# FFN chunks of 502 and 500 columns over the batch border, with attention's result in one DRAM array

## Chip, cores and metric

The kernel runs on one core of a Trainium2 chip. The metric is the device time of one execution in microseconds. A run of the kernel before is the median of three executions; one further execution was profiled.

## What is computed

```python
# u, v: 2 x 3008 x 256; z: 2 x 3008 x 64
scores = (1.0 / S) * np.matmul(z, z.transpose(0, 2, 1))
attn = np.maximum(scores, 0.0) ** 2
x = (u * np.matmul(attn, v)).reshape(B * S, D)      # 6016 x 256
h = np.maximum(x @ moe_w_in, 0.0)                   # 256 -> 2048
x = h * h @ moe_w_out                               # 2048 -> 256
h = x @ moe2_w_in
y = (h - np.tanh(h)) @ moe2_w_out
```

All arrays are float32 in the reference, and the weights arrive as float64. The kernel holds tokens along the free dimension (it reads `u` transposed and writes `y` transposed).

## The kernel before

Every product is computed as three products of a high and a low part: an operand is rounded to the matrix format (`h`), the rest is subtracted (`l`), and TensorE adds high x high, low x high and high x low in PSUM. So each product of a 128-row weight block with a chunk of tokens is three matmuls, each with its own weight load of 128 columns.

**Chunks.** `qch` cuts the 3008 tokens of a batch into five chunks of 512 columns and one of 448. `chunks` lists them for both batches, `NCH` = 12 in all; chunks 5 and 11 (counted from 0) have 448 columns. In the kernel before this list serves attention and the FFNs alike.

**Attention.** For each chunk, 12 steps `("att", c, x)` compute scores, ReLU, square and the product with `v`. `take` adds the result up into an SBUF tile, and `keep` (L482) stores it to a DRAM scratch tile `xd[c]`. For chunk 0 (`EARLY` = 1) `gate` multiplies by `u` before the store; for the others the product with `u` is made after the load, in `split_x`.

**FFNs.** Each FFN has 16 steps per chunk, one for each 128 columns of its hidden dimension: `("m1", c, k)` and `("m2", c, k)`. A step has a front and a back. `front` (L493) is six matmuls (three products over two halves of the 256 features) into a PSUM tile `s`. Between them ScalarE and VectorE compute the nonlinear function and split its result: for m1 `bend` (L519), `power` (L522), `high` (L565 on ScalarE or L567 on VectorE) and `rest` (L570); for m2 `shape` (L528), `bend` (L519), `shape2` (L531), `differ` (L536), `mask` (L547 on VectorE), `times` (L555), `pick` (L558), `high` and `rest`. `back` (L572) is six matmuls of the result into two PSUM tiles `o` that collect all 16 steps. With 12 chunks, 32 steps and 12 matmuls each there are 4608 matmuls in the FFNs.

After its 16 steps an m1 chunk is split into the operand of m2 by `between`, and an m2 chunk is copied out by `out` and stored by `send`. The very last half chunk is copied and stored in two pieces by `send_last` (L630 to L633), one on ScalarE's DMA queue.

**Order.** m1 runs 41 steps ahead of m2 at first (`lead`); later the lead shrinks to 21, and after the last m1 step the last 21 m2 steps stand alone. In these `mask` runs on ScalarE (`alone`, L543). On TensorE the order is written out: the fronts run `LOOK` = 3 steps ahead of the backs, and `FAR` = 4 after the last m1 step. For the other engines and for the SP queue a planner fixes the order while the program is built: each piece of work is a `Job` with a due time, a cost, what it must follow and the buffers it takes, and `drive` always takes the next by these. The due times come from `plan`, which adds up TensorE's times. The order is therefore static, and it depends on the costs that the planner is given. In the kernel before the line that gives the FFN's six matmuls their time is

```python
t += 0.68 * size(i) if kind == "s" else 1.36 if size(i) == 1 else 1.22
```

**Loads for the FFNs.** `load_x` (L262) reads a chunk back from `xd` into a tile of the pool `xp` (two buffers, shared with the output tile `y`); `load_u` (L300) brings its `u`. Their due times lie 16 us before the chunk's first front (`need - 16.0`), and the load may not be issued before that chunk's `keep`.

Of the kernel before, what the change touches and what calls it, by code (L numbers as in the profile page):

```python
# [9 lines left out]
F32 = mybir.dt.float32  # L10
# [7 lines left out]
P = 128  # L18
NMAX = 512
# [12 lines left out]
EARLY = 1  # L32
# [10 lines left out]
def kernel(  # L43
# [22 lines left out]
    B, DQK, S = zT.shape  # L66
    D = v.shape[2]
    DFF = w1_in.shape[1]
    KD = D // P
# [7 lines left out]
    NC = len(qch)  # L77
    chunks = [(b, q, n) for b in range(B) for q, n in qch]
    NCH = len(chunks)
    NV = KB // 2  # L80

    wp = ctx.enter_context(tc.tile_pool(name="wp", bufs=NW))
# [8 lines left out]
    dp = ctx.enter_context(tc.tile_pool(name="dp", bufs=1, space=bass.MemoryType.DRAM))  # L91
# [5 lines left out]
    V, A, T, SP = nc.vector, nc.scalar, nc.tensor, nc.sync  # L97
# [20 lines left out]
    steps = [("att", c, x) for c in range(NCH) for x in range(NV)]  # L118
# [16 lines left out]
    xt = {}  # L135
# [2 lines left out]
    nc.gpsimd.memset(ebias, -float(896 << 23))  # L138
    lbias = cp.tile([P, 1], F32, name="lbias")
    nc.gpsimd.memset(lbias, (TC * math.tanh(TB * TH)) ** 2)  # L140
    xd = dp.tile([NCH, P, KD, NMAX], F32, name="xd")
    wd = dp.tile([KEEP0 + KEEP1, P, 2, 512], F32, name="wd")
    ad = {
        (b, t, k): dp.tile([4, P, 4, P], F32, name="ad")
# [115 lines left out]
        return xs[m, c]  # L260

    def load_x(c):  # L262
        n = chunks[c][2]
        x = xp.tile([P, KD, NMAX], F32, tag="x", name="xr")
        SP.dma_start(out=x[:, :, :n], in_=xd[c, :, :, :n])
        return x

    def split_x(c, x, u):
        n = chunks[c][2]
        if c >= EARLY:  # L270
            yield "V", lambda: V.tensor_mul(x[:, :, :n], x[:, :, :n], u[:, :, :n])
        xh, xl = new_xs(0, c)
        yield "A", lambda: A.activation(xh[:, :, :n], x[:, :, :n], AF.Copy)
        for k in range(KD):
            yield "V", lambda k=k: V.tensor_sub(xl[:, k, :n], x[:, k, :n], xh[:, k, :n])


    order = [(m, f) for m in range(2) for f in range(NF)]
    keeps = {STAY + k: k for k in range(KEEP0 + KEEP1)}
    split = STAY + KEEP0 + KEEP1  # L280
# [16 lines left out]
        k = p % 2 * 2 + g  # L297
        return z[:, k * P : (k + 1) * P]

    def load_u(c, u):  # L300

        b, q, n = chunks[c]
        t0 = b * S + q
        SP.dma_start(
            out=u[:, :, :n],
            in_=uT[:, t0 : t0 + n].rearrange("(k p) t -> p k t", p=P),
        )
# [173 lines left out]

    def keep(c):  # L482

        n = chunks[c][2]
        x = xt.pop(c) if c < EARLY else sums[c]
        SP.dma_start(out=xd[c, :, :, :n], in_=x[:, :, :n])

    def ask_u(c):

        xt[c] = xp.tile([P, KD, NMAX], F32, tag="x", name="x")  # L490
        load_u(c, xt[c])

    def front(i):  # L493
        kind, c, k = steps[i]
        n = chunks[c][2]
        if not single:
            s_pool.close()
            single["s"] = ctx.enter_context(
                tc.tile_pool(name="pf", bufs=4, space=bass.MemoryType.PSUM)
            )  # L500
        s = got[i] = single["s"].tile([P, NMAX], F32, tag="s", name="s")
        m = 0 if kind == "m1" else 1
        w = wt["w", m, k]
        xh, xl = xs[m, c]
        seq = [(hl, mv, kd) for hl, mv in ((0, xh), (1, xh), (0, xl)) for kd in range(KD)]
        for j, (hl, mv, kd) in enumerate(seq):
            T.matmul(  # L507
                s[:, :n],
                lhsT=w[:, hl, kd * P : (kd + 1) * P],
                rhs=mv[:, kd, :n],  # L510
                start=j == 0,
                stop=j == len(seq) - 1,
            )

    def bend(i, func):

        n = chunks[steps[i][1]][2]
        a = sq[i] = ap_.tile([P, NMAX], F32, tag="a", name="a")[:, :n]
        A.activation(a, got[i][:, :n], func)  # L519

# [2 lines left out]

    def shape(i):

        n = chunks[steps[i][1]][2]
        f = gs[i] = fs[i] = tp.tile([P, NMAX], F32, tag="t", name="f")[:, :n]
        A.activation(f, got[i][:, :n], AF.Tanh, scale=TB)  # L528

# [2 lines left out]

    def differ(i):

        n = chunks[steps[i][1]][2]
        V.tensor_sub(sq[i], got[i][:, :n], sq[i])  # L536

    def mask(i, alone):

        n = chunks[steps[i][1]][2]  # L540
        if alone:
            small = zp.tile([P, 2, KD, NMAX], F32, tag="z", name="least")[:, 0, 0, :n]
            A.activation(small, fs[i], AF.Relu, scale=-1.0, bias=lbias)  # L543
            least[i] = small.bitcast(U32)
        else:
            small = least[i] = mp.tile([P, NMAX], U8, tag="small", name="small")[:, :n]
            V.tensor_scalar(small, fs[i], limit, None, op0=ALU.is_lt)  # L547

    def times(i, alone):

        n = chunks[steps[i][1]][2]
        f = fs[i]
        if alone:
            gs[i] = tp.tile([P, NMAX], F32, tag="t", name="g")[:, :n]
        V.tensor_mul(gs[i], got[i][:, :n], f)  # L555
# [3 lines left out]

    def high(i, e, pool):  # L560

        n = chunks[steps[i][1]][2]
        pair[i] = pool.tile([P, 2, NMAX], F32R, tag="h" if pool is hp else "w", name="h")[:, :, :n]
        if e == "A":
            A.activation(pair[i][:, 0], sq[i], AF.Copy)  # L565
        else:
            V.tensor_copy(pair[i][:, 0], sq[i])  # L567
# [3 lines left out]

    def back(i):  # L572
        kind, c, k = steps[i]
        n = chunks[c][2]
        if k == 0:
            acc[kind, c] = [po.tile([P, NMAX], F32, tag="o", name="o") for _ in range(KD)]
        o = acc[kind, c]
        w = wt["w", 0 if kind == "m1" else 1, k]
        h, l = pair[i][:, 0], pair[i][:, 1]
        seq = [(t, d) for t in ((0, h), (1, h), (0, l)) for d in range(KD)]  # L580
        if k in (0, NF - 1):
            seq.sort(key=lambda x: x[1])
        for j, ((side, mv), d) in enumerate(seq):
            T.matmul(  # L584
                o[d][:, :n],
                lhsT=w[:, side, (KD + d) * P : (KD + d + 1) * P],
                rhs=mv,
                start=k == 0 and j % 3 == 0,
                stop=k == NF - 1 and j % 3 == 2,
            )  # L590

    def between(c, d, e):

        n = chunks[c][2]
        if d == 0 and e == "A":
            new_xs(1, c)
        xh, xl = xs[1, c]
        o = acc["m1", c][d][:, :n]
        if e == "A":
            A.activation(xh[:, d, :n], o, AF.Copy)  # L600
        else:
            V.tensor_sub(xl[:, d, :n], o, xh[:, d, :n])

    def out(c, d, e):

        n = chunks[c][2]
        if d == 0:
            xt["y", c] = xp.tile([P, KD, NMAX], F32, tag="x", name="y")
        y, o = xt["y", c][:, d, :n], acc["m2", c][d][:, :n]
        if e == "A":  # L610
            A.activation(y, o, AF.Copy)
        else:
            V.tensor_copy(y, o)

    def send(c):

        b, q, n = chunks[c]
        t0 = b * S + q
        SP.dma_start(
            out=yT[:, t0 : t0 + n].rearrange("(k p) t -> p k t", p=P),  # L620
            in_=xt["y", c][:, :, :n],
        )

    def send_last():

        c = NCH - 1
        b, q, n = chunks[c]
        t0 = b * S + q
        y, o = xt["y", c], acc["m2", c]
        SP.dma_start(out=yT[:P, t0 : t0 + n], in_=y[:, 0, :n])  # L630
        for way, cols in ((A, slice(0, n // 2)), (SP, slice(n // 2, n))):
            V.tensor_copy(y[:, 1, cols], o[1][:, cols])  # L632
            way.dma_start(out=yT[P:, t0 : t0 + n][:, cols], in_=y[:, 1, cols])  # L633
# [136 lines left out]
    def span(kind, i):  # L770
# [2 lines left out]
            return whole  # L773
        return whole * (share if kind == "o" else 1 - share)

    def plan(first_steps):

        order_p, ahead = [], 2
# [18 lines left out]
                ahead += 1  # L797
            order_p.append(("b", n))
        when, t = {}, 0.0
        size = lambda i: chunks[steps[i][1]][2] / NMAX  # L800
        for kind, i in order_p:
            when[kind, i] = t
            if kind[0] == "o":
                t += size(i) * span(kind, i)
            else:
                t += 0.68 * size(i) if kind == "s" else 1.36 if size(i) == 1 else 1.22
        vjob, zjob, blocks = {}, {}, {}
        zhold = {(b, t): hold("z") for b in range(B) for t in range(0, NC, 2)}
        vhold = {(b, j): hold("w") for b in range(B) for j in range(NV)}
# [31 lines left out]
        for b in range(B):  # L841
            base = b * NC * NV
            for j in range(NV):
# [7 lines left out]
                if b == 0 and j in v_loaded:  # L851
                    raw[0] = v_loaded[j]
                    room[pool].pop(0)
                    after = [(asked[0], 3.0 + 0.5 * j)]
                else:
# [4 lines left out]
                    after = [(load, 0.0)]  # L860
# [84 lines left out]
        for c in range(NCH):  # L945
# [8 lines left out]
            def ask2(e, pools, c=c, u=u):  # L954
                pool = homes[pools[0]]
                u[0] = pool.tile([P, KD, NMAX], F32, tag=pools[0], name="u")
                load_u(c, u[0])
            after = [(asks, 0.0), (("keep", c), 0.0)]
            after = [(Job(ask, need - 16.0, after, ["x"], [xs_], S=2.6), 0.0)]
            X = [("A", 1.06), ("V", 0.69), ("V", 0.69)]  # L960
            give = [(2, xs_)]
# [23 lines left out]
    def forward(kind, c, k, when, size, wjob, whold, xjob, xhold):  # L985
# [2 lines left out]
        m, f = int(kind == "m2"), size(i)  # L988
        alone = i > at["m1", NCH - 1, NF - 1]
        need = when["b", i]  # L990
        part = 1.36 if f == 1 else 1.22
        s_, a, t_, small, hs = hold("f"), hold("a"), hold("t"), hold("z" if alone else "small"), hold(None)
        after = [(wjob[m, k], 0.0), *xjob[m, c]]
        if i == at["m1", 0, 0]:
# [62 lines left out]
        y = hold("x")  # L1057
# [208 lines left out]
```

## Time and profile before

| | us |
|---|---|
| median of three executions | 1474.54 |
| lowest and highest of the three | 1474.37 and 1474.82 |
| the profiled execution, whole | 1474.81 |
| its span, first to last instruction | 1473.0 |

The profiled execution is thus 0.27 us above the median, and 1.81 us of it lie outside the span. The span has attention in its first part and the FFNs from about 442 us on. TensorE's row in the profile counts overlapping matmuls as one busy time and models their ends, so its work is read here from start times: the distance from one matmul's start to the next one's.

### The profile page before, as it was taken

The numbers are of one execution on the slowest core, as the hardware profiler recorded it, in microseconds if no ns is written. First come the engines' busy times: TensorE is split into PE (matmuls) and PEld (weight loads), VectorE is DVE, ScalarE is ACT, GpSimd is POOL, SyncE is SP. The second block draws the span as 40 slices with busy tenths as digits, with TensorE's granted clock in tenths as the row PEclk, the third lists the DMA queues.
The fourth block names the chain that finished last, engine by engine and source line by source line (L and its number), as shares of the span: only waits on it lengthen the run. The fifth ranks groups of instructions, "written<-read, shape, count | busy, mean of one in ns | idle before, by whom it ended". The sixth has DMA issues, their size and how long they took to land.

```text
span 1473.0 us, 21953 instructions
## 1 busy us (share of the span) xinstructions
PE 1467.4 (100%) x8512; PEld 1232.4 (84%) x8512; DVE 1230.8 (84%) x1837; ACT 1078.8 (73%) x1712; POOL 0.3 (0%) x6
## 2 busy tenths in 40 slices
PE   9999999999999999999999999999999999999999
PEld 7888888888898888888888888888888888888888
DVE  7888999788986888877888888887888878888888
ACT  8987659987648987666667667677766766666688
POOL 0000000000000000000000000000000000000000
PEclk9999999999999999999999999999999999999999
DMA  8756548765663330010100100010101010000000
GB/s 247 254 191 221 208 154 259 268 219 211 216 243 103 111 95 35 1 40 1 44 1 0 44 1 15 1 44 1 41 1 43 1 40 1 15 1 1 15 1 28
DMA packets 71784, 125.67 MB, mean 85 GB/s; under 512 B 4736, under 2 KB 52224, under 8 KB 67840
## 3 DMA queue, kind: packets, MB, share of 16 engines
q1 hardware_dynamic: 71376, 123.90, 24.8%
q8 instruction: 66, 1.08, 0.3%
q10 hardware_dynamic: 304, 0.38, 0.1%
q14 instruction: 38, 0.31, 0.1%
HBM read 75.24 MB, written 49.02 MB: 84 GB/s over the span
## 4 chain that ended last, share of the span: by engine, by line
PE 99%; DMA 1%; SPq 0%; DVE 0%; issue 0%; DVEq 0%
PE o L584 35%; PE s L507 35%; PE o L458 25%; PE s L421 4%; DMA vraw<-in_v_dram 0%; DMA zraw<-in_z_dram 0%; SPq L180 0%; SPq L160 0%; DVE l L363 0%; DVE vw L173 0%; DVE y L632 0%; DVEq L1262 0%
## 5 line engine op out<-in xcount | busy, mean ns | idle before, releaser
L584 PE MATMUL o<-h,ww 128*128 128x512 f32 (+1 forms) x2304 | 575.6, 385 | 0.0
L507 PE MATMUL s<-xs,ww 128*128 128x512 f32 (+1 forms) x2304 | 575.2, 385 | 0.0
L584 PEld LDWEIGHTS o<-h,ww 128*128 128x128 f32 x2304 | 432.3, 188 | 81.4 <-DVE h L570 0.3
L507 PEld LDWEIGHTS s<-xs,ww 128*128 128x128 f32 x2304 | 432.4, 188 | 81.3 <-issue 0.3
L458 PE MATMUL o<-h,vw 64*128 64x512 f32 (+1 forms) x2256 | 341.4, 382 | 0.2 <-ACT vw L172 0.2
L519 ACT ACTIVATE a<-s 128x512 f32<-128x512 f32 (+1 forms) x384 | 225.1, 586 | 153.4 <-PE s L507 152.1
L570 DVE TENSOR_TENSOR h<-a,h 128x512 fp32r<-128x512 f32 (+1 forms) x384 | 249.4, 677 | 28.3 <-ACT h L565 24.6
L458 PEld LDWEIGHTS o<-h,vw 64*128 64x128 f32 x2256 | 211.4, 184 | 40.5 <-ACT vw L172 0.7
L536 DVE TENSOR_TENSOR a<-s,a 128x512 f32<-128x512 f32 (+1 forms) x192 | 130.3, 679 | 109.4 <-ACT a L519 109.0
L458 PE MATMUL o<-l,vw 64*128 64x512 f32 (+1 forms) x1128 | 215.5, 383 | 0.4 <-DVE l L363 0.4
L528 ACT ACTIVATE f<-s 128x512 f32<-128x512 f32 (+1 forms) x192 | 112.9, 588 | 106.6 <-PE s L507 105.5
L565 ACT ACTIVATE h<-a 128x512 fp32r<-128x512 f32 (+1 forms) x230 | 142.0, 619 | 22.0 <-PE o L584 10.7
L558 DVE COPY_PREDICATED a<-small,f 128x512 f32<-128x512 uint8 (+1 forms) x171 | 126.8, 742 | 5.2
L458 PEld LDWEIGHTS o<-l,vw 64*128 64x128 f32 x1128 | 105.4, 184 | 21.8 <-DVE l L363 1.7
L522 ACT ACTIVATE a<-a 128x512 f32<-128x512 f32 (+1 forms) x192 | 119.5, 622 | 5.3
L329 DVE STREAM_TRANSPOSE at<-m 128x1024 f32<-128x1024 f32 x60 | 121.4, 2023 | 0.0
L555 DVE TENSOR_TENSOR f<-s,f 128x512 f32<-128x512 f32 (+1 forms) x171 | 117.0, 684 | 5.1
L531 ACT ACTIVATE f<-f 128x512 f32<-128x512 f32 (+1 forms) x192 | 120.1, 626 | 0.0
L363 DVE TENSOR_TENSOR l<-a,h 128x1024 fp32r<-128x1024 f32 (+1 forms) x83 | 100.5, 1214 | 20.7 <-ACT h L354 20.3
L354 ACT ACTIVATE h<-at 128x1024 fp32r<-128x1024 f32 (+1 forms) x60 | 61.4, 1023 | 47.7 <-PE o L458 42.2
L385 ACT ACTIVATE a<-a 128x1024 f32<-128x1024 f32 (+1 forms) x83 | 87.3, 1053 | 1.3
L374 ACT ACTIVATE a<-s 128x1024 f32<-128x1024 f32 x79 | 80.0, 1014 | 6.7 <-PE s L421 6.3
(56 smaller groups left out, 801.7 us busy)
## 6 DMA issues: line engine op xcount, KB each, us to landing
ad<-a SPq DMA_DIRECT2D x60, 512.0 KB, 3.9
m<-ad SPq DMA_DIRECT2D x30, 1024.0 KB, 6.7
wraw<-in_moe_w_in_dram SPq DMA_DIRECT2D x32, 256.0 KB, 3.9
wraw<-in_moe_w_out_dram SPq DMA_DIRECT2D x32, 256.0 KB, 4.1
vraw<-in_v_dram SPq DMA_DIRECT2D x22, 256.0 KB, 5.0
wd<-wk SPq DMA_DIRECT2D x10, 512.0 KB, 3.8
ww<-wd SPq DMA_DIRECT2D x10, 512.0 KB, 9.2
xr<-xd SPq DMA_DIRECT2D x10, 512.0 KB, 4.7
```

The source lines that it names most:

```text
L329: V.transpose(a.rearrange("p g (k j m) -> p m k g j", k=4, m=4), m.rearrange("p (m k) (t g i) -> t p m k g i", m=4, t=2, g=2)[p % 2],)
L458: T.matmul(o[r * KD + d][:, :n], lhsT=w[halves[r], hl, g * D + d * P : g * D + (d + 1) * P], rhs=mv[halves[r], g, :n], start=x == 0 and (r ...
L507: T.matmul(s[:, :n], lhsT=w[:, hl, kd * P : (kd + 1) * P], rhs=mv[:, kd, :n], start=j == 0, stop=j == len(seq) - 1,)
L519: A.activation(a, got[i][:, :n], func)
L522: A.activation(sq[i], sq[i], AF.Square)
L531: A.activation(fs[i], fs[i], AF.Square, scale=TC)
L536: V.tensor_sub(sq[i], got[i][:, :n], sq[i])
L555: V.tensor_mul(gs[i], got[i][:, :n], f)
L558: V.copy_predicated(sq[i], least[i], gs[i])
L565: A.activation(pair[i][:, 0], sq[i], AF.Copy)
L570: V.tensor_sub(pair[i][:, 1], sq[i], pair[i][:, 0])
L584: T.matmul(o[d][:, :n], lhsT=w[:, side, (KD + d) * P : (KD + d + 1) * P], rhs=mv, start=k == 0 and j % 3 == 0, stop=k == NF - 1 and j % 3 ...
```

## The change

The FFNs get a chunking of their own. `groups` cuts the 6016 tokens of both batches together into twelve chunks: eight of 502 columns and four of 500. The sixth group (tokens 2510 to 3011) lies over the batch border at 3008. Attention keeps its chunks of 512 and 448.

The scratch `xd` becomes one array over all tokens. `keep` writes an attention chunk into its columns, `load_x` reads a group's columns; a group's load now follows the `keep` of every attention chunk that it touches. Since chunk 0 is already multiplied by `u` and covers 512 tokens, group 1 leaves out its first 10 columns in that product. The planner's time for six FFN matmuls becomes a formula of the width.

```diff
+    assert B * S % 2 == 0
+    even = [2 * (B * S // 2 // NCH + (c < B * S // 2 % NCH)) for c in range(NCH)]
+    groups = [(sum(even[:c]), n) for c, n in enumerate(even)]
+
+    def width(kind, c):
+        return chunks[c][2] if kind == "att" else groups[c][1]
...
-    xd = dp.tile([NCH, P, KD, NMAX], F32, name="xd")
+    xd = dp.tile([P, KD, B * S], F32, name="xd")
...
     def load_x(c):
-        n = chunks[c][2]
+        t0, n = groups[c]
         x = xp.tile([P, KD, NMAX], F32, tag="x", name="xr")
-        SP.dma_start(out=x[:, :, :n], in_=xd[c, :, :, :n])
+        SP.dma_start(out=x[:, :, :n], in_=xd[:, :, t0 : t0 + n])
...
         if c >= EARLY:
-            yield "V", lambda: V.tensor_mul(x[:, :, :n], x[:, :, :n], u[:, :, :n])
+            y = slice(max(done_u - t0, 0), n)
+            yield "V", lambda: V.tensor_mul(x[:, :, y], x[:, :, y], u[:, :, y])
...
     def keep(c):
-        n = chunks[c][2]
+        b, q, n = chunks[c]
+        t0 = b * S + q
         x = xt.pop(c) if c < EARLY else sums[c]
-        SP.dma_start(out=xd[c, :, :, :n], in_=x[:, :, :n])
+        SP.dma_start(out=xd[:, :, t0 : t0 + n], in_=x[:, :, :n])
...
     def front(i):
         kind, c, k = steps[i]
-        n = chunks[c][2]
+        n = groups[c][1]
...
+    def ffn(f):
+        return 0.08 + 1.28 * f
...
-        size = lambda i: chunks[steps[i][1]][2] / NMAX
+        size = lambda i: width(*steps[i][:2]) / NMAX
...
-                t += 0.68 * size(i) if kind == "s" else 1.36 if size(i) == 1 else 1.22
+                t += 0.68 * size(i) if kind == "s" else ffn(size(i))
...
-                load_u(c, u[0])
-            after = [(asks, 0.0), (("keep", c), 0.0)]
+                load_u(*groups[c], u[0])
+            t0, n = groups[c]
+            after = [(asks, 0.0)]
+            for k, (b, q, m) in enumerate(chunks):
+                if t0 < b * S + q + m and b * S + q < t0 + n:
+                    after.append((("keep", k), 0.0))
...
-        part = 1.36 if f == 1 else 1.22
+        part = ffn(f)
```

The other functions of the FFNs (`bend` to `rest`, `back`, `between`, `out`, `send`, `send_last`) take their width, and the last two their tokens, from `groups` in the same way.

## Rows read from the trace of the kernel before

**Rows 1.** The page's busy times by engine, and the granted clock by slice.

```profile
PE 1467.4 (100%) x8512; PEld 1232.4 (84%) x8512; DVE 1230.8 (84%) x1837; ACT 1078.8 (73%) x1712; POOL 0.3 (0%) x6
...
PEclk9999999999999999999999999999999999999999
```

**Rows 2.** The page's chain that ended last, by engine.

```profile
PE 99%; DMA 1%; SPq 0%; DVE 0%; issue 0%; DVEq 0%
```

**Rows 3.** Instructions of lines 507 and 584: count, durations (ns), first and last start (us).

```profile
L507 PE MATMUL s<-xs,ww x2304: 362/389/506, 442.0 to 1462.9; 128*128 128x512 f32 x157, 128*128 128x448 f32 x35
...
L584 PE MATMUL o<-h,ww x2304: 362/389/468, 447.6 to 1469.2; 128*128 128x512 f32 x157, 128*128 128x448 f32 x35
```

**Rows 4.** TensorE's timeline where all FFN chunks have 512 columns: start, length, six matmuls each.

```profile
599.94 1.52 PE L584 MATMUL o<-h,ww 128*128 128x512 f32 x6
...
610.82 1.52 PE L584 MATMUL o<-h,ww 128*128 128x512 f32 x6
```

**Rows 5.** The same timeline in the last chunk, 448 columns alone.

```profile
1436.35 1.38 PE L584 MATMUL o<-h,ww 128*128 128x448 f32 x6
...
1461.89 1.38 PE L507 MATMUL s<-xs,ww 128*128 128x448 f32 x6
```

**Rows 6.** Weight loads of line 507 over the span: busy time, mean ns, idle before.

```profile
L507 PEld LDWEIGHTS s<-xs,ww 128*128 128x128 f32 x2304 | 432.4, 188 | 81.3 <-issue 0.3
```

**Rows 7.** TensorE's timeline where chunks of 448 and 512 columns alternate.

```profile
765.86 1.52 PE L584 MATMUL o<-h,ww 128*128 128x512 f32 x6
767.22 1.38 PE L507 MATMUL s<-xs,ww 128*128 128x448 f32 x6
768.43 1.54 PE L584 MATMUL o<-h,ww 128*128 128x512 f32 x6
769.82 1.52 PE L507 MATMUL s<-xs,ww 128*128 128x512 f32 x6
```

**Rows 8.** Timeline at the FFNs' start, all engines.

```profile
442.04 5.75 PE L507 MATMUL s<-xs,ww 128*128 128x512 f32 x24
...
447.62 1.52 PE L584 MATMUL o<-h,ww 128*128 128x512 f32 x6
```

**Rows 9.** Busy us of PE, PEld, DVE, ACT, POOL by stretch, then clock, DMA, GB/s.

```profile
560.00:760.00 200.00, 200.00 (x884) 165.58 (x884) 161.54 (x270) 135.84 (x236) 0.00 (x0) 1.00 0.05 18
...
1422.00:1462.00 40.00, 40.00 (x194) 36.17 (x194) 39.62 (x74) 39.38 (x81) 0.00 (x0) 1.00 0.04 14
```

**Rows 10.** Groups of two operations over 1422 to 1462 us, by form.

```profile
L558 DVE COPY_PREDICATED a<-least,g 128x448 f32<-128x448 uint32 x14 | 9.6, 682 | 0.0
L543 ACT ACTIVATE least<-f,lbias 128x448 f32<-128x448 f32 x14 | 9.5, 677 | 0.3
...
L558 DVE COPY_PREDICATED a<-least,g 128x512 f32<-128x512 uint32 x3 | 2.3, 761 | 0.0
L543 ACT ACTIVATE least<-f,lbias 128x512 f32<-128x512 f32 x3 | 2.2, 729 | 0.0
```

**Rows 11.** Timeline of the last 6 us; in brackets the idle time before and its releaser.

```profile
1467.69 1.53 PEld L584 LDWEIGHTS o<-h,ww 128*128 128x128 f32 x8 [0.34 <-DVE h L570]
...
1469.63 0.69 DVE L632 COPY y<-o 128x224 f32<-128x224 f32 x2 [1.17 <-PE o L584]
1470.06 0.35 ACTq L633 DMA_DIRECT2D out_dram<-y  x1
1470.35 0.34 SPq L633 DMA_DIRECT2D out_dram<-y  x1
```

**Rows 12.** The stores of line 486: count, issue durations (ns), first and last start (us).

```profile
L486 SPq DMA_DIRECT2D xd<-e x11: 319/320/596, 89.9 to 443.4; - x11
```

**Rows 13.** DMA issues by form: count, KB each, median us to landing.

```profile
xr<-xd SPq DMA_DIRECT2D x10, 512.0 KB, 4.7
out_dram<-y SPq DMA_DIRECT2D x10, 512.0 KB, 3.1
...
out_dram<-y SPq DMA_DIRECT2D x1, 112.0 KB, 1.9
```

More of the change, by code (lines that the diff above doesn't have):

```diff
@@ L275, in split_x @@
             yield "V", lambda k=k: V.tensor_sub(xl[:, k, :n], x[:, k, :n], xh[:, k, :n])
+    done_u = sum(n for _, _, n in chunks[:EARLY])
     order = [(m, f) for m in range(2) for f in range(NF)]
@@ L298, in keys, with load_u @@
         return z[:, k * P : (k + 1) * P]
-    def load_u(c, u):
-        b, q, n = chunks[c]
-        t0 = b * S + q
+    def load_u(t0, n, u):
         SP.dma_start(
@@ L482, in keep @@
     def keep(c):
-        n = chunks[c][2]
+        b, q, n = chunks[c]
+        t0 = b * S + q
         x = xt.pop(c) if c < EARLY else sums[c]
-        SP.dma_start(out=xd[c, :, :, :n], in_=x[:, :, :n])
+        SP.dma_start(out=xd[:, :, t0 : t0 + n], in_=x[:, :, :n])
     def ask_u(c):
         xt[c] = xp.tile([P, KD, NMAX], F32, tag="x", name="x")
-        load_u(c, xt[c])
+        b, q, n = chunks[c]
+        load_u(b * S + q, n, xt[c])
     def front(i):
         kind, c, k = steps[i]
-        n = chunks[c][2]
+        n = groups[c][1]
         if not single:
@@ L515, in bend @@
     def bend(i, func):
-        n = chunks[steps[i][1]][2]
+        n = width(*steps[i][:2])
         a = sq[i] = ap_.tile([P, NMAX], F32, tag="a", name="a")[:, :n]
@@ L524, in shape @@
     def shape(i):
-        n = chunks[steps[i][1]][2]
+        n = width(*steps[i][:2])
         f = gs[i] = fs[i] = tp.tile([P, NMAX], F32, tag="t", name="f")[:, :n]
@@ L533, in differ @@
     def differ(i):
-        n = chunks[steps[i][1]][2]
+        n = width(*steps[i][:2])
         V.tensor_sub(sq[i], got[i][:, :n], sq[i])
     def mask(i, alone):
-        n = chunks[steps[i][1]][2]
+        n = width(*steps[i][:2])
         if alone:
@@ L549, in times @@
     def times(i, alone):
-        n = chunks[steps[i][1]][2]
+        n = width(*steps[i][:2])
         f = fs[i]
@@ L560, in high @@
     def high(i, e, pool):
-        n = chunks[steps[i][1]][2]
+        n = width(*steps[i][:2])
         pair[i] = pool.tile([P, 2, NMAX], F32R, tag="h" if pool is hp else "w", name="h")[:, :, :n]
@@ L573, in back @@
         kind, c, k = steps[i]
-        n = chunks[c][2]
+        n = groups[c][1]
         if k == 0:
@@ L592, in between @@
     def between(c, d, e):
-        n = chunks[c][2]
+        n = groups[c][1]
         if d == 0 and e == "A":
@@ L604, in out @@
     def out(c, d, e):
-        n = chunks[c][2]
+        n = groups[c][1]
         if d == 0:
@@ L615, in send @@
     def send(c):
-        b, q, n = chunks[c]
-        t0 = b * S + q
+        t0, n = groups[c]
         SP.dma_start(
@@ L626, in send_last @@
         c = NCH - 1
-        b, q, n = chunks[c]
-        t0 = b * S + q
+        t0, n = groups[c]
         y, o = xt["y", c], acc["m2", c]
@@ L956, in ask2 @@
                 u[0] = pool.tile([P, KD, NMAX], F32, tag=pools[0], name="u")
-                load_u(c, u[0])
-            after = [(asks, 0.0), (("keep", c), 0.0)]
+                load_u(*groups[c], u[0])
+            t0, n = groups[c]
+            after = [(asks, 0.0)]
+            for k, (b, q, m) in enumerate(chunks):
+                if t0 < b * S + q + m and b * S + q < t0 + n:
+                    after.append((("keep", k), 0.0))
             after = [(Job(ask, need - 16.0, after, ["x"], [xs_], S=2.6), 0.0)]
```

## The prediction

> **What bounds the kernel now.** I read the page first. TensorE is busy for practically the whole span, at full granted clock in every slice; VectorE and ScalarE are not [rows 1]. The chain of waits says the same from the other end: 99% of it is TensorE [rows 2]. So the time is the sum of the matmuls' own times plus the few places where TensorE waits, and the change can gain only by making matmuls cheaper or removing such places. It concerns the FFNs' 4608 matmuls alone.
>
> The lengths in TensorE's rows are modelled, so I read distances between starts. The FFNs' first matmul starts at 442.0 and the last at 1469.2 [rows 3]; with 0.2 for the last one itself the FFNs hold TensorE for 1027.4 us. To see what that is made of I asked for TensorE's timeline in three kinds of stretch.
>
> Where all chunks have 512 columns, eight groups of six matmuls lie between the first row and the last: (610.82 - 599.94) / 48 = 226.67 ns each [rows 4]. At the granted clock of 1.00, the 2.4 GHz level [rows 9], 512 columns are 213.33 ns, so 13.33 ns per matmul are not columns.
>
> In the last chunk, with 448 columns alone, 21 groups lie between the rows: (1461.89 - 1436.35) / 126 = 202.70 ns [rows 5]. The same composition would give 448 / 2.4 + 13.33 = 200.00. What is longer there is the weight load. It lasts 188 ns whatever the chunk [rows 6], and 188 + 14.7 = 202.7: under a matmul of 448 columns it no longer fits. Under one of 512 it has 226.67 - 188 = 38.7 ns to spare.
>
> Where the two widths alternate, a chunk of 448 also taxes its neighbour. A group of six 512s that follows one of 448 takes 769.82 - 768.43 = 1.39 us, while the group before the 448s took 767.22 - 765.86 = 1.36 [rows 7].
>
> **The change part by part.** *Twelve even chunks instead of ten wide and two narrow.* The number of matmuls stays 4608 and the columns stay 384 x 6016. If a matmul costs columns / 2.4 + 13.33 ns, the FFNs cost 384 x 6016 / 2.4 = 962.56 us, plus 4608 x 13.33 = 61.44, together 1024.0, however the tokens are cut. The kernel before is 3.4 above this line. Of that, 768 matmuls of 448 columns make 768 x 2.70 = 2.07. The start makes 0.14: the first 24 matmuls take 447.62 - 442.04 = 5.58 instead of 5.44 [rows 8]. The end makes about 0.3, where the weight loads wait for VectorE's `h` [rows 11]. The rest, 0.9, I put down to the neighbours of [rows 7].
>
> At 500 and 502 columns the line gives 221.67 and 222.50 ns. The weight load then has 33.7 ns to spare, near the 38.7 at which no excess shows, and far from the 448s. So the 2.07 and the 0.9 go. The start and the end stay. New sum: 1024.0 + 0.14 + 0.34 = 1024.5, a gain of 2.9.
>
> The width itself does not occur in the trace, so I bound it from the two that do. If nothing of a matmul were fixed, its price would be 226.67 / 512 per column. At the mean width of 501.33 that is 221.94 ns, and 1022.7 us in all: 1.3 less than the line. If the price lay on the straight line between the two measured widths it would be 202.70 + 53.33 x 23.97 / 64 = 222.67, and 1026.1 in all: 2.1 more. I take the line of fixed part and clock between them, since the 448s are explained by the weight load and so say little about the slope.
>
> *The end of the kernel.* The last chunk grows from 448 to 500 columns. After the last matmul stand two copies of half a chunk and their stores [rows 11]. The copies take 0.69 for 224 columns each; 250 columns make it 0.69 x 250 / 224 = 0.77, so +0.08. The last store moves 125 KB instead of 112. It lands in 1.9 us [rows 13], so between nothing and 0.2 more. I take 0.02, because an output of 512 KB lands in 3.1. Together +0.1.
>
> *VectorE and ScalarE.* While m1 and m2 steps alternate they have room: 162 and 136 of 200 us [rows 9], and 502 columns are less work than 512. In the last 21 m2 steps, which stand alone, they have none: 39.6 and 39.4 of 40 [rows 9]. There, from 448 to 500 columns `pick` grows by 52 x (761 - 682) / 64 = 64 ns or 9%, and `mask` by 42 ns or 6% [rows 10]. TensorE's matmul grows from 202.70 to 221.67, by 9%. So the engines keep pace as they do now, and I cost this at nothing. The cover is TensorE's own lead of four fronts. Were it used up, what comes late is the next `back`, and the price is the second rival.
>
> *Moved loads and stores.* No DMA is added. `keep` writes rows of 2 KB into the array instead of 4 KB. The last one is issued at 443.4 [rows 12] and, by the store of equal size, lands some 3 us later [rows 13]. Only the last two groups need it. The first group needs chunk 0's `keep` alone, as before, and the sixth those of three chunks that were stored hundreds of us earlier. Were a group's load to wait for a store that it does not need, SP's queue behind it, with the weights' loads, would stand for those 3 us. Loads are due 16 us ahead and land in 4.7 [rows 13], so that hides it. Without that cover it would cost 3 us once.
>
> A rule that speaks against the change concerns these rows. Off a 512-column grid, a group's rows start at multiples of 2008 bytes. The Trainium skill, "DMA: Bandwidth & Descriptors", section "How a descriptor splits into AXI transactions", says that a piece which does not start on a 256-byte boundary also fetches the bytes before it. Estimated from that page, the last rows' 1000 bytes cost 33 beats, where the 896 bytes of before cost 28. No row here shows an unaligned piece of this kind. By the page the last store's data would take up to 18% longer, which stays inside the 0.2 allowed for it, and the loads keep their cover.
>
> *Sum.* -2.9 + 0.1 = -2.8 us. The profiled execution took 1474.81 us with a span of 1473.0, and this makes it 1472.0 with a span of 1470.2. That execution is 0.27 above the median, so the forecast for the median is 1474.54 - 2.8 = **1471.7 us**. That is 0.19% less. About 0.2% (2.95 us) is what a measurement of this kernel can tell from no change, so the forecast lies just inside that limit.
>
> **Rivals.**
>
> *The array works in steps of columns.* Both measured widths are multiples of 64, so the trace can't exclude that 502 and 500 columns are charged as the next multiple of something. With a step of 16 or more both cost what 512 does: 4608 x 226.67 = 1044.5, which is 20.5 above the line and gives 1492.2, slower by 1.2%. From a step of 16 on this decides the sign; with a step of 8 (504 columns for both, 223.33 ns) it is 1029.1, so 5.1 more and 1476.8; with 4, 1474.3. Nothing in the rows speaks for it. Against it speaks only that 512 columns need no more than their clocks plus a small remainder. The Trainium skill, "TensorE: Matmul & The Clock Gate", section "Wait — 56ns, not 53.3ns?", gives a matmul's distance as columns over the clock plus 2.5 ns, without steps. The trace differs in the constant (13.3), and no run here shows a width off the grid.
>
> *The last steps, or a new static order, stall TensorE.* The planner gets new costs and so may set another order. Both helpers are full in the last 52 us, and the kernel before already ends with 0.34 us of waiting for `h` [rows 9, 11]. If each of the 21 steps came late by a tenth of its 2.66 us, that is 5.6 us and 1477.3; half of that gives 1474.5. Against it: 162 of 200 before that stretch, and equal growth in it.
>
> *The narrow chunks were not the cause.* If price per column between 448 and 512 is a straight line, the 2.07 us stay and only the neighbours' tax goes: 1471.7 + 2.1 = 1473.8, no change to be told. The weight load's 188 ns speak against it.
>
> **How the numbers follow.** The forecast's own case, a smooth price per column and no new stall, gets 0.78; within it the time lies from 1470.4 to 1472.7. Its fixed part decides whether it passes the 0.2% limit, at 1471.6: I give 0.43 to faster and 0.35 to same. A column step of 16 or more gets 0.05 (slower), of 4 or 8 together 0.05 (same). The stalls get 0.08, of which 0.06 same and 0.02 slower. The straight line gets 0.04 (same). Together: faster 0.43, same 0.50, slower 0.07. The range must leave out no more than 0.2. I take 1470.2 to 1474.3; this holds the forecast's case, the straight line, a step of 4 and the small stalls.
>
> **What would show it.** Right: starts of matmuls 221.7 and 222.5 ns apart through all of the FFNs, no group of 1.39 us, first to last start near 1023.9 + 0.4, and attention's part as before, its last matmul near 442. Wrong: 226.7 or 223.3 ns per matmul; weight loads or matmuls waiting for `h` in the last 50 us for more than 0.5 us; TensorE waiting for an `xs` of a new group; or a last store that lands later than 2.1 us.

## The result, and the profile after

The changed kernel takes 1483.23 us (median of six, 1482.62 to 1483.81), the kernel before in the same runs 1474.68. The ratio is 1.0059, with a 95% interval of 1.0048 to 1.0070: slower by 8.6 us, where 2.8 less was forecast and the range ended at 1474.3. Three executions in the experiments below ran at a granted clock of 0.62 to 0.85, among them the profiled ones of `e3_array_only` and `e7_narrow_last`; the ratios leave them out, and no row of their traces is used.

The page of the changed kernel, busy times and chain, says what it said before [rows 1, 2]: TensorE is the bound.

```profile
PE 1474.8 (100%) x8512; PEld 1232.5 (83%) x8512; DVE 1237.9 (84%) x1851; ACT 1072.1 (72%) x1698; POOL 0.3 (0%) x6
...
PE 98%; DMA 1%; DVE 0%; SPq 0%; issue 0%; ACT 0%; DVEq 0%
```

The FFNs' matmuls (now lines 516 and 593), with first and last start:

```profile
L516 PE MATMUL s<-xs,ww x2304: 382/385/502, 441.4 to 1469.6; 128*128 128x502 f32 x125, 128*128 128x500 f32 x67
...
L593 PE MATMUL o<-h,ww x2304: 382/388/498, 446.9 to 1477.1; 128*128 128x502 f32 x125, 128*128 128x500 f32 x67
```

From first to last start the FFNs take 1035.7 us, against 1027.2 before [rows 3]. They begin 0.6 earlier, and after the last start stand 4.2 us instead of 3.8. 8.5 - 0.6 + 0.4 = 8.3 is the difference of the two spans (1481.3 and 1473.0). The 0.6 is no work of the change: in the whole kernels below, which all keep attention as it is, this start lies anywhere from 441.1 to 442.2. So the loss is in the FFNs, and TensorE's timeline shows it in stretches without any waiting. Groups of six matmuls, first with 502 columns throughout, then where 502 and 500 alternate, then with 500:

```profile
599.68 1.50 PE L593 MATMUL o<-h,ww 128*128 128x502 f32 x6
...
610.40 1.50 PE L593 MATMUL o<-h,ww 128*128 128x502 f32 x6
...
1147.74 1.50 PE L593 MATMUL o<-h,ww 128*128 128x502 f32 x6
1149.09 1.51 PE L516 MATMUL s<-xs,ww 128*128 128x500 f32 x6
1150.44 1.56 PE L593 MATMUL o<-h,ww 128*128 128x502 f32 x6
1151.83 1.56 PE L516 MATMUL s<-xs,ww 128*128 128x502 f32 x6
1153.23 1.51 PE L593 MATMUL o<-h,ww 128*128 128x500 f32 x6
...
1299.86 1.52 PE L593 MATMUL o<-h,ww 128*128 128x500 f32 x6
...
1310.74 1.52 PE L593 MATMUL o<-h,ww 128*128 128x500 f32 x6
```

(610.40 - 599.68) / 48 = 223.33 ns for 502 columns, and (1310.74 - 1299.86) / 48 = 226.67 ns for 500. The narrower matmul is the dearer one and costs exactly what 512 columns did [rows 4]. Where the two alternate, most groups take 1.34 to 1.36 us. But behind a single group of 500 columns, as the one at 1149.09, the next groups of 502 take 1.39 and 1.40 us, the latter 1.40 / 6 = 233 ns per matmul. That happens behind nine of the ten such single groups, to 19 groups of 502, and costs 1.1 us in all.

The end, in the same order as [rows 11]:

```profile
1474.01 3.02 PEld L593 LDWEIGHTS o<-h,ww 128*128 128x128 f32 x14 [0.78 <-DVE h L579]
1474.01 3.45 PE L593 MATMUL o<-h,ww 128*128 128x500 f32 x14 [0.36 <-DVE h L579]
...
1477.49 0.74 DVE L639 COPY y<-o 128x250 f32<-128x250 f32 x2 [1.45 <-PE o L593]
1477.94 0.35 ACTq L640 DMA_DIRECT2D out_dram<-y  x1
1478.27 0.34 SPq L640 DMA_DIRECT2D out_dram<-y  x1
```

The weight loads wait 0.78 us for `h` (0.34 before). The copies take 0.74 (0.69). By the DMA issues the last store lands after 2.2 us instead of 1.9, and the loads of `x` after 5.0 instead of 4.7 [rows 13]:

```profile
xr<-xd SPq DMA_DIRECT2D x8, 502.0 KB, 5.0
...
out_dram<-y SPq DMA_DIRECT2D x1, 125.0 KB, 2.2
```

### The profile page after: what moved, and what is told of

Its sections match the earlier page's. It is cut to its first block, busy times and chain, and to the rows that moved or that the text cites. A ratio compares the mean times of both kernels' runs of the same rounds, so it can differ in the third digit from the quotient of the medians.

```text
span 1481.3 us, 21975 instructions
## 1 busy us (share of the span) xinstructions
PE 1474.8 (100%) x8512; PEld 1232.5 (83%) x8512; DVE 1237.9 (84%) x1851; ACT 1072.1 (72%) x1698; POOL 0.3 (0%) x6
## 4 chain that ended last, share of the span: by engine, by line
PE 98%; DMA 1%; DVE 0%; SPq 0%; issue 0%; ACT 0%; DVEq 0%
PE s L516 35%; PE o L593 35%; PE o L465 25%; PE s L428 4%; DMA vraw<-in_v_dram 0%; DMA zraw<-in_z_dram 0%; SPq L187 0%; DVE vw L180 0%; DVE l L370 0%; DVE z L204 0%; SPq L167 0%; DVE a L567 0%; DVE h L579 0%; ACT f L537 0%; DVE g L564 0%
## 5 line engine op out<-in xcount | busy, mean ns | idle before, releaser
L593 PE MATMUL o<-h,ww 128*128 128x502 f32 (+1 forms) x2304 | 580.1, 387 | 0.4 <-DVE h L579 0.4
L516 PE MATMUL s<-xs,ww 128*128 128x502 f32 (+1 forms) x2304 | 578.3, 386 | 0.0
L528 ACT ACTIVATE a<-s 128x502 f32<-128x502 f32 (+1 forms) x384 | 226.4, 589 | 162.5 <-PE s L516 161.2
L579 DVE TENSOR_TENSOR h<-a,h 128x502 fp32r<-128x502 f32 (+1 forms) x384 | 249.3, 678 | 15.1 <-ACT h L574 10.5
L545 DVE TENSOR_TENSOR a<-s,a 128x502 f32<-128x502 f32 (+1 forms) x192 | 130.3, 679 | 119.9 <-ACT a L528 118.7
L574 ACT ACTIVATE h<-a 128x502 fp32r<-128x502 f32 (+1 forms) x220 | 138.0, 629 | 23.4 <-PE o L593 13.7
L567 DVE COPY_PREDICATED a<-small,f 128x502 f32<-128x502 uint8 (+1 forms) x171 | 126.1, 737 | 5.1
L531 ACT ACTIVATE a<-a 128x502 f32<-128x502 f32 (+1 forms) x192 | 119.3, 623 | 5.5
L540 ACT ACTIVATE f<-f 128x502 f32<-128x502 f32 (+1 forms) x192 | 121.5, 633 | 0.0
L564 DVE TENSOR_TENSOR f<-s,f 128x502 f32<-128x502 f32 (+1 forms) x171 | 116.2, 679 | 5.0
```

The costliest lines, as they stand in the source:

```text
L516: T.matmul(s[:, :n], lhsT=w[:, hl, kd * P : (kd + 1) * P], rhs=mv[:, kd, :n], start=j == 0, stop=j == len(seq) - 1,)
L531: A.activation(sq[i], sq[i], AF.Square)
L540: A.activation(fs[i], fs[i], AF.Square, scale=TC)
L567: V.copy_predicated(sq[i], least[i], gs[i])
L579: V.tensor_sub(pair[i][:, 1], sq[i], pair[i][:, 0])
L593: T.matmul(o[d][:, :n], lhsT=w[:, side, (KD + d) * P : (KD + d + 1) * P], rhs=mv, start=k == 0 and j % 3 == 0, stop=k == NF - 1 and j % 3 ...
```

## Experiments

Price here means the distance from one matmul's start to the next one's. Theory 1: the price of these matmuls is no smooth function of the width. Theory 2, the rival: the price is the forecast's line, and something around the matmuls (the DRAM array, groups over the border, odd widths on the other engines) stretches them.

**The array alone** (`e3_array_only`).

```diff
-    groups = [(sum(even[:c]), n) for c, n in enumerate(even)]
+    groups = [(b * S + q, n) for b, q, n in chunks]
```

> The changed kernel with the FFNs' groups set to attention's chunks (512 and 448 columns), so that the one array in DRAM is all that remains of the change. If the widths cost the time: 1474.6, the kernel before within 1 us. If the array's loads and stores do: near 1483.

1474.35 us against 1474.37, ratio 1.000 (0.999 to 1.001). The array costs nothing.

**Matmuls alone, by width** (`e1_widths`). The whole kernel is one stream of matmuls on operands copied from `u`; the rest of the work is left out. Each kernel of this kind was executed once, at a granted clock of 1.00:

```python
def run(n, groups):
    for g in range(groups):
        for j in range(6):
            i = (g * 6 + j) % 8
            T.matmul(o[g % 4][:, :n], lhsT=ww[:, i * P : (i + 1) * P],
                     rhs=xs[:, j % 2, :n], start=j == 0, stop=j == 5)
run(512, 8)
for n in (512, 510, 508, ..., 482, 480, 472, 464, 456, 448):
    run(n, 16)
```

> Leaves the whole computation out but matmuls: 96 matmuls (with their weight loads) of each of 21 widths from 512 down to 448 columns, after one another, with no other engine at work. Theory 1, the price of a matmul is not a line over its width, and the matmul stream alone makes it: starts 226.7 ns apart at 512 and at 500, about 223.3 at 502. Theory 2, the price is the line columns / 2.4 + 13.33 and in the changed kernel something around the matmuls (reads and writes of odd widths by the other engines, rows of the array off a grid) stretches it: 222.5 at 502 and 221.7 at 500 here, and one line over all widths down to about 450.

TensorE's timeline at the first two matmuls of the blocks with 504, 502, 500 and 498 columns; a block has 96:

```profile
107.76 0.61 PE L73 MATMUL o<-xs,ww 128*128 128x504 f32 x2
...
129.54 0.62 PE L73 MATMUL o<-xs,ww 128*128 128x502 f32 x2
...
150.99 0.61 PE L73 MATMUL o<-xs,ww 128*128 128x500 f32 x2
...
172.75 0.61 PE L73 MATMUL o<-xs,ww 128*128 128x498 f32 x2
```

(129.54 - 107.76) / 96 = 226.9 ns, then 223.4, then 226.7. Fourteen of the 21 blocks (512 from its part at full clock; the starts are here taken in whole ns, which moves a price by up to 0.1), and what is over columns / 2.4:

```
columns     512   508   504   502   500   498   496   492   490   488   480   472   464   448
ns        226.7 227.7 226.8 223.5 226.6 226.7 223.3 222.2 220.0 225.7 216.7 213.3 208.9 202.6
over      13.3  16.0  16.8  14.3  18.3  19.2  16.7  17.2  15.8  22.4  16.7  16.6  15.6  15.9
```

No other engine is at work here, and 502 and 500 cost what they cost in the changed kernel, so theory 2 falls. The part that isn't columns runs from 13.3 to 22.4 ns without order, and 512 has the least.

**The same widths after others** (`e2_orders`).

> The same kernel of matmuls alone, with the widths in the order 502, 500, 504, 502, 512, 500, 448, 502, 448, 500, 496, 502, 504, 500, 488, 502, 500, 502, so that each width follows different ones. If the price belongs to the width, 500 shows one distance wherever it stands, and 502 one. If the matmuls fall into a rhythm that depends on what ran before, the same width shows two or more distances, such as 223 and 227 for 500, or 223 and 233 for 502.

Starts of two blocks of 500 columns and of the blocks that follow them:

```profile
41.95 0.61 PE L73 MATMUL o<-xs,ww 128*128 128x500 f32 x2
63.39 0.62 PE L73 MATMUL o<-xs,ww 128*128 128x504 f32 x2
...
360.62 0.61 PE L73 MATMUL o<-xs,ww 128*128 128x500 f32 x2
382.37 0.61 PE L73 MATMUL o<-xs,ww 128*128 128x502 f32 x2
```

The first block takes 21.44 / 96 = 223.3 ns per matmul, the other 226.6. Over five blocks 500 showed 223.3 three times and the dearer price twice; 488 gave 220.0 here and 225.7 in the sweep. 502 and 504 came out alike wherever they stood. So some widths hold either of two rhythms. What chooses isn't shown: the block just before does not settle it, since both blocks above follow one of 502. In the changed kernel the 500s fell into the dear one.

**Other widths in the whole kernel.** Three kernels change one line, `even`: `[504] * 8 + [496] * 4` (`e4_504_496`), `[502] * 11 + [494]` (`e8_502_494`), `[512] * 8 + [480] * 4` (`e11_512_480`).

> The changed kernel with eight groups of 504 and four of 496 columns, multiples of 8 that add up to the same 6016. If the price goes in steps of 8 columns and both widths lie on the grid: matmuls 223.3 and 220.0 ns apart, 1024 us of FFN and about 1472. If it goes in steps of 16: 504 costs 226.7 and the time is about 1482. If anything but 512 and 448 is slow because of its rows or because groups cross the border: about 1483, as the changed kernel.

> The changed kernel with eleven groups of 502 and one of 494 columns, so that no group of 500 is left. By the distances of the sweep (223.4 and 223.3) the FFNs take 384 x 12 x 223.4 = 1029.4 us, plus about 1.2 at start and end, which gives about 1478, 5 us under the changed kernel. If the 500s are not what is slow, and evenness, the border or the array is: 1483.

> The changed kernel with eight groups of 512 and four of 480 columns. By the distances measured alone (226.67 and 216.65) the FFNs take 384 x (8 x 226.67 + 4 x 216.65) = 1029.1 us, 1.7 more than the kernel before: 1476 to 1477. On the straight line (222.5 and 213.3 plus nothing else) the FFNs would take 1024.0 and the kernel 1471.7.

| | us | before | ratio (interval) | FFNs, first to last start | 384 x sum of the sweep's prices |
|---|---|---|---|---|---|
| 504 and 496 | 1486.69 | 1474.37 | 1.0084 (1.0067 to 1.0101) | 1039.6 | 1039.7 |
| 502 and 494 | 1477.26 | 1474.45 | 1.0018 (1.0009 to 1.0028) | 1029.6 | 1029.8 |
| 512 and 480 | 1476.27 | 1474.38 | 1.0014 (1.0004 to 1.0023) | 1029.1 | 1029.3 |

The first is dearer than all its expectations: 504 costs 226.7 as on a grid of 16, and 496, which lies on that grid, 223.3 as in the sweep. The two others came out within 0.8 us of what the sweep foretold. The four 500s account for most of the loss: without them it is 2.8 us.

**Narrow groups last** (`e7_narrow_last`, `even = [512] * 10 + [448] * 2`).

> The changed kernel with groups of ten times 512 and then twice 448 columns, cut over the border. By the measured distances 384 x (10 x 226.67 + 2 x 202.6) is the kernel before; what is less is the alternation of 512 and 448, which by the first trace costs the 512s 1.0 us in all. So 1473.9 to 1474.5. If groups that lie over the border or off attention's chunks cost something by themselves: above 1476.

1474.24 against 1474.45, ratio 0.9998 (0.9989 to 1.0007): groups over the border cost nothing, and less alternation gives nothing that can be told.

**Shorter weight loads and another type.** The sweep over 13 of the widths with 64 (`e5_half_weights`) and 32 columns of weights (`e10_quarter_weights`; the output has as many rows), and in bf16 (`e6_bf16`).

```diff
-lhsT=ww[:, i * P : (i + 1) * P]
+lhsT=ww[:, i * P : i * P + 64]
```

> Matmuls alone, as in the sweep over widths, but each loads only 64 columns of weights, so that a weight load should last about half of 188 ns. If the steps and the two rhythms come from the next weight load meeting the matmul that runs, they go, and the distance becomes a line over the width: columns / 2.4 plus one constant at 512, 504, 502, 500, 496 and 480 alike. If the array takes its moving columns in blocks, the steps stay: 504 and 512 alike, 500 no cheaper than 502.

> Matmuls alone with 32 columns of weights each. With 64 columns (a load of 136 ns) the steps had moved but not gone: 500 columns at 220.2, 502 at 232.7, 504 at 230.5. If the weight load's reading meets the moving columns' and delays them, a still shorter load changes the distances once more, and at several widths brings them nearer to columns / 2.4 + 2.5, the line that bf16 keeps (510 ns-columns: 211.7 at 502). If the steps belong to the 4-byte moving columns alone, the distances are those of the 64-column weights.

> The same sweep with 128 columns of weights and both operands in bf16 (the products lose their precision). If the steps belong to the 4-byte format (its weight load or its reads), they go and the distance is columns / 2.4 plus a constant, below 220 at 512. If the array takes columns in blocks whatever the type, 504 still costs what 512 does.

The weight loads by form, first with 64 columns, then with 32:

```profile
L73 PEld LDWEIGHTS o<-xs,ww 128*64 128x64 f32 x1296 | 175.5, 136 | 119.7 <-ACT xs L67 6.8 <-issue 2.2
```

```profile
L73 PEld LDWEIGHTS o<-xs,ww 128*32 128x32 f32 x1296 | 140.9, 109 | 154.9 <-ACT xs L67 7.2 <-issue 3.1
```

The bf16 sweep, starts of four blocks:

```profile
60.80 0.59 PE L73 MATMUL o<-xs,ww 128*128 128x504 bf16 x2
...
81.19 0.59 PE L73 MATMUL o<-xs,ww 128*128 128x502 bf16 x2
...
101.52 0.58 PE L73 MATMUL o<-xs,ww 128*128 128x500 bf16 x2
...
121.75 0.58 PE L73 MATMUL o<-xs,ww 128*128 128x498 bf16 x2
```

```
ns at columns         504   502   500   496   480   472   448   weight load
4 bytes, 128 cols   226.8 223.5 226.6 223.3 216.7 213.3 202.6   188
4 bytes, 64 cols    230.5 232.7 220.2 224.9 216.7 213.3 202.2   136
4 bytes, 32 cols    226.7 226.7 226.7 220.3 216.7 213.5 202.2   109
bf16, 128 cols      212.5 211.7 210.8 209.2 202.5 199.2 189.2    98
```

In bf16 every width lies on columns / 2.4 + 2.5: 20.39 / 96 = 212.4 ns for 504. That part of the expectation held. With the 4-byte operands the steps stay under loads of little more than half the length, and at 480, 472 and 448 they move by no more than 0.4 ns; at 496 to 504 they do move, down as well as up. So neither of the sharp alternatives holds. The steps come with the 4-byte operands, and the weight load only shifts some of them. Whether it is the weights' type or the moving columns' is not shown: the bf16 sweep changes both, and its loads are a little shorter still (98 ns against 109).

**Where the columns start** (`e9_offsets`, `rhs=xs[:, j % 2, x : x + n]`, full weights).

> Matmuls alone with full weights, widths 504, 502, 500 and 480, each with its moving columns starting 0, 2, 8, 12, 16 and 64 columns into the tile; 12 matmuls of 512 columns ahead of each. If the reads are taken in aligned blocks, the distance depends on where the columns start: 480 from column 8 would touch one block more than from 0, and 500 from column 12 would end on a grid of 512. If only the number of columns and the weight loads matter, each width shows the distances that it showed from column 0 (226.7; 223.4; 223.3 or 226.6; 216.7) at every start.

480 columns from 0, from 8 and from 12 (84 matmuls a block), each with the start of the block behind it:

```profile
415.22 0.59 PE L73 MATMUL o<-xs,ww 128*128 128x480 f32 x2
433.42 0.61 PE L73 MATMUL o<-xs,ww 128*128 128x512 f32 x2
...
456.85 0.60 PE L73 MATMUL o<-xs,ww 128*128 128x480 f32 x2
475.33 0.61 PE L73 MATMUL o<-xs,ww 128*128 128x512 f32 x2
478.05 0.59 PE L73 MATMUL o<-xs,ww 128*128 128x480 f32 x2
495.98 0.63 PE L73 MATMUL o<-xs,ww 128*128 128x512 f32 x2
```

18.20 / 84 = 216.7 ns from 0, 220.0 from 8, 213.4 from 12. From 16 it is 218.4, and from 64 it is 216.6 again, as from 0; 504, 502 and 500 too repeat at 64 what they showed at 0. 504 columns from 2 take 230.0 instead of 226.7. So the price hangs on where the columns lie as well as on how many they are. A grid of 16 columns does not explain it: from 8 and from 12, 480 columns touch the same 31 blocks of 16 and differ by 6.6 ns.

**The start column in the whole kernel** (`e12_start12`, `e13_start8`), on top of 512 and 480:

```diff
-        xs[m, c] = (both[:, 0], both[:, 1])
+        x = 12 if groups[c][1] < NMAX else 0
+        xs[m, c] = (both[:, 0, :, x:], both[:, 1, :, x:])
...
-        pair[i] = pool.tile([P, 2, NMAX], F32R, ...)[:, :, :n]
+        pair[i] = pool.tile([P, 2, NMAX], F32R, ...)
+        x = 12 if n < NMAX else 0
+        pair[i] = pair[i][:, :, x : x + n]
```

> Eight groups of 512 and four of 480 columns as before this, but the FFN operands of the 480 groups are laid 12 columns into their tiles, where the matmuls alone stood 213.4 ns apart instead of 216.7. If the distance follows the columns' start also in the whole kernel: FFNs of 384 x (8 x 226.67 + 4 x 213.4) = 1024.1 us and 1471 to 1472, under the kernel before by some 3 us. If it is the width alone, or the order of the work around it: 1476.3 as with start 0.

> The same kernel with the operands of the 480 groups 8 columns into their tiles, where the matmuls alone stood 220.0 ns apart: FFNs of 384 x (8 x 226.67 + 4 x 220.0) = 1034.2 us and 1481 to 1482. If the start column is nothing in the whole kernel: 1476.3.

With start 12 the kernel takes 1472.67 against 1474.40, ratio 0.9989 (0.9980 to 0.9997); with start 8, 1481.74, ratio 1.0050 (1.0037 to 1.0063). TensorE's timeline in the 480 groups, eight groups of six, first from 12, then from 8:

```profile
1301.13 1.44 PE L517 MATMUL s<-xs,ww 128*128 128x480 f32 x6
...
1311.37 1.44 PE L517 MATMUL s<-xs,ww 128*128 128x480 f32 x6
```

```profile
1300.99 1.48 PE L517 MATMUL s<-xs,ww 128*128 128x480 f32 x6
...
1311.55 1.48 PE L517 MATMUL s<-xs,ww 128*128 128x480 f32 x6
```

10.24 / 48 = 213.3 and 10.56 / 48 = 220.0 ns. The two kernels differ in the start of the moving columns alone, and 9.1 us lie between them. Start 12 is the first version that beats both the kernel before and the changed one, the former by 1.7 us: little, but outside the interval. It missed its expected 1471 to 1472 by 0.7. Its FFNs take 1025.3 us from first to last start instead of 1024.1: groups of 512 columns right behind 480 take 229.2 ns per matmul (0.5 us in all), and the last matmuls again wait for `h`, where the distance between two starts is 0.6 us longer than else:

```profile
1463.86 2.86 PEld L596 LDWEIGHTS o<-h,ww 128*128 128x128 f32 x14 [0.83 <-DVE h L582]
1463.86 3.25 PE L596 MATMUL o<-h,ww 128*128 128x480 f32 x14 [0.43 <-DVE h L582]
```

## Why the prediction was wrong

**What bounds the kernel: right.** The FFNs' length followed from the distances of matmuls in every whole kernel whose trace is read above.

**"At 500 and 502 columns the line gives 221.67 and 222.50 ns": this is the step that failed.** Measured are 226.67 and 223.33, the two numbers that the prediction named as signs of being wrong. With 384 matmuls per chunk, the four chunks of 500 and the eight of 502 columns make 1536 x 5.0 + 3072 x 0.83 = 7.68 + 2.55 = 10.2 us of the 11.5 between forecast and result. The bounds failed with it. They joined two measured widths by a smooth curve, 1022.7 to 1026.1 us of FFN; the two widths alone came to 1034.2. Of the 8.6 us lost against the kernel before, 6.0 go when 502 and 494 columns take the place of the 500s (`e8_502_494`).

**"The 448s are explained by the weight load": wrong.** The sum 188 + 14.7 fitted by chance; the 14.7 was only what was left over. With a load of 109 ns, 448 columns still take 202.2. What made 448 dearer than the line belongs to the 4-byte operands as at every other width, and so the 2.07 us had no reason to go.

**Neighbours: only half right.** The tax at 448 went, and one between 502 and 500 came (up to 233 ns). Start, end and alternation together make 1035.9 - 1034.2 = 1.7 us of the changed kernel, against the 0.14 + 0.34 kept in the sum. The 19 groups of 502 at 233 ns make 1.1 of them.

**The end: right in kind, too small.** Copies and store made the tail 0.4 longer instead of 0.1; the store lands 0.3 later, outside the 0.2 allowed. The wait for `h` grew by 0.44. That is the second rival, at a small fraction of its price.

**Loads, stores, the other engines: right on what they cost.** No matmul waits for a group's `xs`, and the array alone takes what the kernel before takes. Only the last group, not the last two, needs the last `keep`; nothing hung on it. The estimate of 33 beats against 28 for the last rows was miscounted: these are the numbers of the first of the two last pieces. Counted the same way from an output array that starts on a 256-byte boundary, the second, which lands last, has 32 before and after, so the trace before did hold such a piece. Both pieces land 0.3 us later (1.8 to 2.1 and 1.9 to 2.2), and 18% of the whole 1.9 us would have been 0.34, not inside the 0.2.

**The rivals.** The first, steps of columns, is the one that came true, though not as a step of one size: 500 columns cost what 512 do, 502 what a step of 8 would make of them, 504 cost 226.7. Its prices for steps of 8 and of 16, 1476.8 and 1492.2, enclose the result. I gave it 0.10 in all, because nothing in the rows spoke for it; but two widths, both multiples of 64, could not have. The straight line kept the 2.07 us and, at 1473.8, got the sign wrong too.

What makes the steps inside the array stays open. The runs show that they need 4-byte operands, that the columns' start moves them and that they repeat at a start of 64, that the weight load shifts some of them, and that one width can hold either of two rhythms; not how these meet.

## What to carry to other kernels

When TensorE is the bound, measure the price of a new matmul shape in a short stream of matmuls before cutting the work anew; a price between two measured widths is not known, and the same cut can gain or lose with the column in which the operands start. Equal chunks are no gain in themselves: the 512s of the kernel before had the cheapest fixed part of all widths measured from column 0 with full weights. A duration that fits a gap is a guess until it has been changed.

## What the runs showed of the hardware

- At the 2.4 GHz level, bf16 matmuls with 128 weight columns keep columns / 2.4 + 2.5 ns at all of the 12 widths from 448 to 508. The Trainium skill, "TensorE: Matmul & The Clock Gate", section "Wait — 56ns, not 53.3ns?", states this sum, and the bf16 run agrees (212.5 ns at 504). In the 4-byte format (float32r) the remainder is 13.3 to 22.4 ns instead, not monotone in the width.
- Start and width act together: 480 columns of 4 bytes take 213.4, 216.7 or 220.0 ns from columns 12, 0 and 8, and in the whole kernel 213.3 and 220.0 from 12 and 8.
- Some widths hold two steady rhythms over a block of 96 matmuls: 500 at 223.3 or 226.6 ns, 488 at 220.0 or 225.7. In the changed kernel 502 columns take 223.3 ns, but 232.5 and then 233.3 in the groups behind a single group of 500, nine times out of ten.
- Weight loads last 188, 136 and 109 ns for 128, 64 and 32 columns in 4 bytes, and 98 for 128 in bf16.
